# A fused Linformer-attention and MLP-mixer kernel: fixed program order with interleaved front steps, crossbar turns, and a down-projection from seven quadrant products

## The chip, the cores and the metric

One core of a Trainium2 chip runs the kernel. The metric is device time in microseconds (us) of one execution, as a median over runs. The profile is one execution, traced; its span (first to last instruction) is some 2 us shorter than the time of that execution. Engines: PE is TensorE, PEld its weight load, DVE VectorE, ACT ScalarE, POOL GpSimd, SP the queue of SyncE.

## The reference

Eight batches, each 1024 tokens x 512 channels (8 heads of 64). Attention first projects K and V along the sequence to 64 rows, so the scores of a head are 1024 x 64. The result goes through a token mixing (1024 to 256 to 1024, with a residual) and a channel MLP (512 to 1536 to 512, with a residual).

```python
k_proj = einsum('ks,bhsd->bhkd', E, k);  v_proj = einsum('ks,bhsd->bhkd', F, v)
attn   = softmax(q @ k_proj.T / 8)                  # max subtraction left out in both kernels
x      = (attn @ v_proj)  -> [B, S, H*D]
u      = x + (relu(x.T @ w_tok1) @ w_tok2).T        # token mixing
out    = u + relu(u @ w_ch1) @ w_ch2                # up- and down-projection
```

I call attention plus token mixing of a batch its *front*, and up- plus down-projection its *main* part.

## The kernel before

The body is written batch by batch; the framework's scheduler orders the instructions by priority and by what is ready. Operands are bf16, sums fp32 in PSUM.

```python
def attention(b):
    ...                                             # k, v, q loaded head by head, cast to bf16
    for hp in range(HP):                            # q: re-laid by a copy, turned on TensorE
        nc.any.tensor_copy(out=q2_sb[:, hp], in_=q_sb[...])
    for hp in range(HP):
        for sj in range(2):
            for ss in range(4):
                nc.tensor.transpose(qt_ps[:, ss * P : (ss + 1) * P], q2_sb[...], ident)
            nc.vector.tensor_copy(out=qT_sb[...], in_=qt_ps)
    for si in range(NSI):                           # V, then the same for K
        nc.tensor.matmul(vproj_ps, FT_sb[:, si, :], v_sb[:, :, si, :], ...)
    ...
            for ss in range(4):                     # denominators and outputs: 2 matmuls each
                nc.tensor.matmul(dn_ps[:, 2*ss : 2*ss+2], lhs, bd_ones, ...)
                nc.tensor.matmul(ou_ps[:, ss, :], lhs, vbd_sb[:, hp, :], ...)
    ...
def mixer(b, x_sb):
    ...                                             # token mixing: h_ps, u_ps, u_sb
                    nc.tensor.transpose(ut_ps[...], u_sb[:, sc, dc * P : (dc + 1) * P], ident)
                nc.vector.tensor_copy(out=uT_sb[...], in_=ut_ps)
    for sj in range(2):
        for cc in range(CC):                        # up: 96 matmuls of 512 columns a batch
            ...
            nc.any.tensor_relu(out=gT_sb[:, cc, s_lo : s_lo + S2], in_=gT_ps)
    for sc in range(SC):
        for cc in range(CC):                        # down: 96 matmuls of 512 columns a batch
            nc.tensor.matmul(g2_ps, gT_sb[:, cc, sc*P:(sc+1)*P], wc2_sb[:, cc, :], ...)
        nc.vector.tensor_add(out=o_sb, in0=g2_ps, in1=u_sb[:, sc, :])
        nc.sync.dma_start(out=..., in_=o_sb)
...
for b in range(B):
    if b + 1 < B: xs[b + 1] = attention(b + 1)
    mixer(b, xs[b])
```

Of the kernel before, what the change touches and what calls it, by code (L numbers as in the profile page):

```python
# [11 lines left out]
AX = mybir.AxisListType  # L12
ALU = mybir.AluOpType
ACT = mybir.ActivationFunctionType


@with_exitstack
def kernel(
# [14 lines left out]
    P = 128  # L33

# [5 lines left out]

    SC = S // P
    NSI = SC
    TC = DT // P
    DMC = DM // P
    CC = DC // P
    HP = H // 2
    scale = 1.0 / (D ** 0.5)
    S2 = S // 2

    const = ctx.enter_context(tc.tile_pool(name="const", bufs=1))  # L50
    wpool = ctx.enter_context(tc.tile_pool(name="weights", bufs=1))
    kv_pool = ctx.enter_context(tc.tile_pool(name="kv", bufs=2))
    attn_small = ctx.enter_context(tc.tile_pool(name="attn_small", bufs=4))
    attnT_pool = ctx.enter_context(tc.tile_pool(name="attnT", bufs=8))
    qT_pool = ctx.enter_context(tc.tile_pool(name="qT", bufs=2))
    mix_pool = ctx.enter_context(tc.tile_pool(name="mix", bufs=2))
    gT_pool = ctx.enter_context(tc.tile_pool(name="gT", bufs=1))
    out_pool = ctx.enter_context(tc.tile_pool(name="outp", bufs=4))
    psA = ctx.enter_context(tc.tile_pool(name="psA", bufs=8, space=bass.MemoryType.PSUM))
    dram_pool = ctx.enter_context(tc.tile_pool(name="dram", bufs=3, space=bass.MemoryType.DRAM))  # L60

    ident = const.tile([P, P], BF16)
    make_identity(nc, ident)
    bd_ones = const.tile([P, 2], BF16)
    nc.vector.memset(bd_ones, 0.0)
    nc.vector.memset(bd_ones[0:KP, 0:1], 1.0)
    nc.vector.memset(bd_ones[KP : 2 * KP, 1:2], 1.0)

    E_sb = const.tile([KP, S], BF16)
    nc.gpsimd.dma_start(out=E_sb, in_=E)  # L70
    F_sb = const.tile([KP, S], BF16)
    nc.gpsimd.dma_start(out=F_sb, in_=F)
    ET_sb = wpool.tile([P, SC, KP], BF16)
    FT_sb = wpool.tile([P, SC, KP], BF16)
    for si in range(NSI):
        ssl = slice(si, S, NSI)
        e_ps = psA.tile([P, KP], BF16, tag="ps", name="e_ps")
        nc.tensor.transpose(e_ps, E_sb[:, ssl], ident[:KP, :KP])
        nc.vector.tensor_copy(out=ET_sb[:, si, :], in_=e_ps)
        f_ps = psA.tile([P, KP], BF16, tag="ps", name="f_ps")  # L80
        nc.tensor.transpose(f_ps, F_sb[:, ssl], ident[:KP, :KP])
        nc.vector.tensor_copy(out=FT_sb[:, si, :], in_=f_ps)

    def attention(b):
        k_sb = kv_pool.tile([P, H, NSI, D], BF16, tag="k_sb", name="k_sb")
        v_sb = kv_pool.tile([P, H, NSI, D], BF16, tag="v_sb", name="v_sb")
        for h in range(H):
            rr = "(p si) d -> p si d"
            nc.gpsimd.dma_start(out=k_sb[:, h, :, :], in_=k[b, h].rearrange(rr, p=P))  # L89
            nc.gpsimd.dma_start(out=v_sb[:, h, :, :], in_=v[b, h].rearrange(rr, p=P))  # L90

        q_sb = kv_pool.tile([P, H, NSI, D], BF16, tag="q_sb", name="q_sb", bufs=1)
        for h in range(H):
            nc.gpsimd.dma_start(  # L94
                out=q_sb[:, h, :, :], in_=q[b, h].rearrange("(p si) d -> p si d", p=P)
            )
        q2_sb = kv_pool.tile([P, HP, NSI, 2, D], BF16, tag="q2_sb", name="q2_sb", bufs=1)
        for hp in range(HP):
            nc.any.tensor_copy(  # L99
                out=q2_sb[:, hp],  # L100
                in_=q_sb[:, 2 * hp : 2 * hp + 2].rearrange("p j si d -> p si j d"),
            )
        qT_sb = qT_pool.tile([P, HP, S], BF16, tag="qT_sb", name="qT_sb")
        for hp in range(HP):
            for sj in range(2):
                qt_ps = psA.tile([P, S2], BF16, tag="ps", name="qt_ps")
                for ss in range(4):
                    si = sj * 4 + ss
                    nc.tensor.transpose(  # L109
                        qt_ps[:, ss * P : (ss + 1) * P],  # L110
                        q2_sb[:, hp, si, :, :].rearrange("p j d -> p (j d)"),
                        ident,
                    )
                nc.vector.tensor_copy(  # L114
                    out=qT_sb[:, hp, sj * S2 : (sj + 1) * S2], in_=qt_ps
                )

        vproj_ps = psA.tile([KP, H, D], F32, tag="ps", name="vproj_ps")
        for si in range(NSI):
            nc.tensor.matmul(  # L120
                vproj_ps, FT_sb[:, si, :], v_sb[:, :, si, :],
                start=(si == 0), stop=(si == NSI - 1),
            )
        vbd_sb = attn_small.tile([P, HP, 2 * D], BF16, tag="vbd_sb", name="vbd_sb")
        nc.gpsimd.memset(vbd_sb, 0.0)
        for hp in range(HP):
            nc.vector.tensor_copy(out=vbd_sb[0:KP, hp, 0:D], in_=vproj_ps[:, 2 * hp, :])
            nc.vector.tensor_copy(  # L128
                out=vbd_sb[KP : 2 * KP, hp, D : 2 * D], in_=vproj_ps[:, 2 * hp + 1, :]
            )  # L130

        kproj_ps = psA.tile([KP, H, D], F32, tag="ps", name="kproj_ps")
        for si in range(NSI):
            nc.tensor.matmul(
                kproj_ps, ET_sb[:, si, :], k_sb[:, :, si, :],
                start=(si == 0), stop=(si == NSI - 1),
            )
        kproj_sb = attn_small.tile([KP, H, D], BF16, tag="kproj_sb", name="kproj_sb")
        nc.vector.tensor_copy(out=kproj_sb, in_=kproj_ps)
        kprojT_sb = attn_small.tile([P, HP, KP], BF16, tag="kprojT_sb", name="kprojT_sb")  # L140
        for hp in range(HP):
            tp_ps = psA.tile([P, KP], BF16, tag="ps", name="tp_ps")
            nc.tensor.transpose(
                tp_ps,
                kproj_sb[:, 2 * hp : 2 * hp + 2, :].rearrange("k j d -> k (j d)"),
                ident[:KP, :KP],
            )
            nc.vector.tensor_copy(out=kprojT_sb[:, hp, :], in_=tp_ps)

        x_sb = mix_pool.tile([P, SC, DM], BF16, tag="x_sb", name="x_sb")  # L150

        for sj in range(2):
            slo = sj * S2
            attns = []
            for hp in range(HP):
                sco_ps = psA.tile([P, S2], F32, tag="ps", name="sco_ps")
                nc.tensor.matmul(
                    sco_ps[0:KP, :], kprojT_sb[0:D, hp, :],
                    qT_sb[0:D, hp, slo : slo + S2], start=True, stop=True,
                )  # L160
                nc.tensor.matmul(  # L161
                    sco_ps[KP : 2 * KP, :], kprojT_sb[D : 2 * D, hp, :],
                    qT_sb[D : 2 * D, hp, slo : slo + S2], start=True, stop=True,
                )
                attnT_sb = attnT_pool.tile([P, S2], BF16, tag="attnT_sb", name="attnT_sb")
                nc.scalar.activation(out=attnT_sb, in_=sco_ps, func=ACT.Exp, scale=scale)  # L166
                attns.append(attnT_sb)
            for hp in range(HP):
                h0 = 2 * hp
                attnT_sb = attns[hp]  # L170
                dn_ps = psA.tile([P, 8], F32, tag="ps", name="dn_ps")
                ou_ps = psA.tile([P, 4, 2 * D], F32, tag="ps", name="ou_ps")
                for ss in range(4):
                    lhs = attnT_sb[:, ss * P : (ss + 1) * P]
                    nc.tensor.matmul(  # L175
                        dn_ps[:, 2 * ss : 2 * ss + 2], lhs, bd_ones, start=True, stop=True
                    )
                    nc.tensor.matmul(  # L178
                        ou_ps[:, ss, :], lhs, vbd_sb[:, hp, :], start=True, stop=True
                    )  # L180
                rdn = attn_small.tile([P, 8], F32, tag="rdn", name="rdn")
                nc.vector.reciprocal(out=rdn, in_=dn_ps)
                nc.vector.tensor_tensor(  # L183
                    out=x_sb[:, sj * 4 : sj * 4 + 4, h0 * D : (h0 + 2) * D]
                    .rearrange("p s (j d) -> p s j d", j=2),
                    in0=ou_ps.rearrange("p s (j d) -> p s j d", j=2),
                    in1=rdn.rearrange("p (s j) -> p s j", j=2)[:, :, :, None]
                    .to_broadcast([P, 4, 2, D]),
                    op=ALU.mult,
                )  # L190
        return x_sb
# [70 lines left out]
    for b in range(B):  # L262
        if b + 1 < B:
            xs[b + 1] = attention(b + 1)
# [32 lines left out]
```

## Time and profile before

| | before |
|---|---|
| time, median of 4 runs | 572.56 us (571.37 to 573.18) |
| span of the profile | 570.8 us |
| until the first up-projection | 85.2 us |
| one batch in the steady part | 64.7 us |
| busy share PE / DVE / ACT | 89% / 37% / 31% |

The page's table of 40 slices, before (each digit is a tenth; a slice is 14.3 us). PE is at 0.9 and more from the seventh slice on, at full clock; the six slices ahead of that are lower. The 9 at the head of the clock row says too much: the trace has no record of the clock before 24.5 us, and the table counts that time as full, but 128-column matmuls there start every 107 ns, as where the record says half clock, and not every 56 as later.

```profile
PE   1540889999999999998999999999999999999997
PEclk9975889999999999999999999999999999999999
```

The chain of waits, before (start, length, what). It returns to the same piece every 64.7 us. `gT_ps` is the up-, `g_ps` the down-projection.

```profile
85.20 20.96 PE gT_ps L233 x96
106.16 20.73 PE g_ps L242 x96
...
214.57 20.96 PE gT_ps L233 x96
235.53 20.73 PE g_ps L242 x96
...
269.40 3.45 PE h_ps L198 x16
...
279.47 20.96 PE gT_ps L233 x96
```

96 matmuls in 20.73 us and 16 in 3.45 us are 216 ns from one start to the next. I call this interval the *pitch*. It is the thing to add up for TensorE: the durations in the profile (379 ns for the same matmuls) overlap.

The timeline of TensorE, before (start, length, instruction, count). The 32 transposes take 1.95 us to the end of the last one (itself 0.22 us), so they start every 56 ns, each with a weight load of its own. The two score matmuls of a pair (L157, L161) use different quarters of the array and start within 10 ns of each other. From the last output matmul to the first score matmul it is 140 ns, where the starts ahead of it follow each other by 30 to 50.

```profile
256.09 1.95 PE L109 MATMUL qt_ps<-ident,q_sb 128*128 128x128 bf16 x32
...
266.14 0.22 PE L178 MATMUL ou_ps<-vbd_sb,attnT_sb 128*128 128x128 bf16 x1
266.28 0.40 PE L157 MATMUL sco_ps<-qT_sb,kprojT_sb 64*64 64x512 bf16 x1
266.29 0.40 PE L161 MATMUL sco_ps<-qT_sb,kprojT_sb 64*64 64x512 bf16 x1
```

### The profile page before, as it was taken

The page shows a single profiled execution, that of the slowest core. Times are in us where ns is not written, and L with a number is a line of the kernel's source. Part 1 is how long each engine was busy: PE and PEld are TensorE (multiplying, and loading weights), DVE is VectorE, ACT ScalarE, POOL GpSimd, SP SyncE. Part 2 cuts the span into 40 slices and gives each one's busy share as a digit, 9 for nine tenths or more (in the row PEclk, how much of TensorE's full clock was granted, in tenths as well). Part 3 has the DMA queues.
Part 4 walks back from the last instruction along what each step waited for, and adds up shares of the span by engine and source line. Part 5 has one row for each costly group of instructions (what it writes and reads, how often), then busy time and mean ns, then how long its engine had stood idle before and what let it go on. Part 6 is the DMA issues. An engine that isn't in the chain of part 4 may idle for free.

```text
span 570.8 us, 7698 instructions
## 1 busy us (share of the span) xinstructions
PE 509.8 (89%) x3120; PEld 259.4 (45%) x3120; DVE 210.4 (37%) x524; ACT 175.9 (31%) x288; POOL 110.9 (19%) x212
## 2 busy tenths in 40 slices
PE   1540889999999999998999999999999999999997
PEld 0330454454544454445544454445544454445443
DVE  1440571137502572028602563027601563025012
ACT  0221336305260235304260235404261034500720
POOL 8608871006200360006200260000000000000000
PEclk9975889999999999999999999999999999999999
DMA  9999992129502390028601391020001200020012
GB/s 135 208 208 202 201 201 44 38 92 151 91 0 79 102 186 4 27 103 134 109 1 73 94 185 19 20 102 28 1 1 69 80 2 0 18 94 38 1 55 92
DMA packets 39555, 46.90 MB, mean 82 GB/s; under 512 B 4192, under 2 KB 30304, under 8 KB 39520
## 3 DMA queue, kind: packets, MB, share of 16 engines
q0 software_dynamic: 30304, 29.63, 32.4%
q1 hardware_dynamic: 9216, 16.78, 7.5%
q8 instruction: 24, 0.39, 0.3%
q14 instruction: 11, 0.09, 0.1%
HBM read 59.24 MB, written 16.78 MB: 133 GB/s over the span
## 4 chain that ended last, share of the span: by engine, by line
PE 71%; DVE 14%; DMA 6%; POOL 5%; issue 2%; ACT 1%; DVEq 0%; ACTq 0%; POOLq 0%
PE gT_ps L233 29%; PE g_ps L242 29%; DVE u_sb L213 6%; PE h_ps L198 5%; DMA wc_sb<-in_moe_w_ch_dram 4%; DVE qT_sb L114 2%; PE ou_ps L178 2%; PE ut_ps L219 2%; POOL v_sb L90 2%; POOL q_sb L94 2%; PE u_ps L209 2%; POOL k_sb L89 1%; DVE x_sb L183 1%; PE dn_ps L175 1%; DVE vbd_sb L128 1%
## 5 line engine op out<-in xcount | busy, mean ns | idle before, releaser
L233 PE MATMUL gT_ps<-uT_sb,wc_sb 128*128 128x512 bf16 x768 | 169.0, 379 | 0.0
L242 PE MATMUL g_ps<-wc_sb,gT_sb 128*128 128x512 bf16 x768 | 167.1, 379 | 0.0
L238 ACT ACTIVATE gT_sb<-gT_ps 128x512 bf16<-128x512 f32 x184 | 109.0, 597 | 111.6 <-PE gT_ps L233 110.5
L247 DVE TENSOR_TENSOR o_sb<-g_ps,u_sb 128x512 f32<-128x512 f32 x64 | 44.3, 692 | 267.7 <-PE g_ps L242 267.7
L242 PEld LDWEIGHTS <-gT_sb 128*128 128x128 bf16 x768 | 75.1, 98 | 90.7
L233 PEld LDWEIGHTS <-wc_sb 128*128 128x128 bf16 x768 | 74.8, 98 | 90.7 <-issue 3.8
L90 POOL DMA_DIRECT2D v_sb<-in_v_dram x64 | 34.7, 545 | 203.2 <-PE vproj_ps L120 188.5
L99 ACT COPY q_sb<-q_sb 128x1024 bf16<-128x1024 bf16 x23 | 23.1, 1044 | 133.8 <-PE qt_ps L109 109.8
L166 ACT ACTIVATE attnT_sb<-sco_ps 128x512 bf16<-128x512 f32 x64 | 33.0, 602 | 61.2 <-PE sco_ps L161 61.2
L109 PE MATMUL qt_ps<-ident,q_sb 128*128 128x128 bf16 x256 | 19.5, 242 | 34.4 <-ACT q_sb L99 34.4
L213 DVE TENSOR_TENSOR u_sb<-u_ps,x_sb 128x512 bf16<-128x512 f32 x64 | 39.0, 683 | 21.2 <-PE u_ps L209 21.2
L183 DVE TENSOR_TENSOR x_sb<-ou_ps,rdn 128x512 bf16<-128x512 f32 x64 | 41.7, 681 | 1.7
L89 POOL DMA_DIRECT2D k_sb<-in_k_dram x64 | 34.6, 554 | 14.9 <-DMA wc_sb<-in_moe_w_ch_dram 6.8
L94 POOL DMA_DIRECT2D q_sb<-in_q_dram x64 | 34.0, 534 | 10.1 <-issue 5.3
L109 PEld LDWEIGHTS <-q_sb 128*128 128x128 bf16 x256 | 17.6, 109 | 37.1 <-ACT q_sb L99 35.5
L114 DVE COPY qT_sb<-qt_ps 128x512 bf16<-128x512 bf16 x64 | 23.0, 417 | 19.2 <-PE qt_ps L109 19.1
L175 PE MATMUL dn_ps<-bd_ones,attnT_sb 128*128 128x2 bf16 x256 | 27.4, 171 | 2.8 <-ACT attnT_sb L166 1.5
L178 PE MATMUL ou_ps<-vbd_sb,attnT_sb 128*128 128x128 bf16 x256 | 29.8, 221 | 0.0
L198 PE MATMUL h_ps<-x_sb,wt_sb 128*128 128x512 bf16 x128 | 29.7, 386 | 0.0
L209 PE MATMUL u_ps<-hT_sb,wt_sb 128*128 128x512 bf16 x128 | 28.9, 379 | 0.0
L175 PEld LDWEIGHTS <-attnT_sb 128*128 128x128 bf16 x256 | 20.0, 96 | 16.2 <-ACT attnT_sb L166 10.8
L219 PE MATMUL ut_ps<-ident,u_sb 128*128 128x128 bf16 x256 | 21.5, 221 | 5.1 <-DVE u_sb L213 4.6
(46 smaller groups left out, 260.0 us busy)
## 6 DMA issues: line engine op xcount, KB each, us to landing
out_dram<-o_sb SPq DMA_DIRECT2D x64, 256.0 KB, 2.0
k_sb<-in_k_dram POOLq DMA_DIRECT2D x64, 128.0 KB, 4.9
v_sb<-in_v_dram POOLq DMA_DIRECT2D x64, 128.0 KB, 4.9
q_sb<-in_q_dram POOLq DMA_DIRECT2D x64, 128.0 KB, 4.9
wc_sb<-in_moe_w_ch_dram POOLq DMA_DIRECT2D x2, 1536.0 KB, 18.8
wt_sb<-in_moe_w_tok_dram POOLq DMA_DIRECT2D x2, 512.0 KB, 7.4
E_sb<-in_E_dram POOLq DMA_DIRECT2D x1, 128.0 KB, 3.1
F_sb<-in_F_dram POOLq DMA_DIRECT2D x1, 128.0 KB, 3.4
```

Source lines behind the costliest of these rows:

```text
L90: nc.gpsimd.dma_start(out=v_sb[:, h, :, :], in_=v[b, h].rearrange(rr, p=P))
L94: nc.gpsimd.dma_start(out=q_sb[:, h, :, :], in_=q[b, h].rearrange("(p si) d -> p si d", p=P))
L175: nc.tensor.matmul(dn_ps[:, 2 * ss : 2 * ss + 2], lhs, bd_ones, start=True, stop=True)
L178: nc.tensor.matmul(ou_ps[:, ss, :], lhs, vbd_sb[:, hp, :], start=True, stop=True)
L183: nc.vector.tensor_tensor(out=x_sb[:, sj * 4 : sj * 4 + 4, h0 * D : (h0 + 2) * D] .rearrange("p s (j d) -> p s j d", j=2), in0=ou_ps.rearr ...
L198: nc.tensor.matmul(h_ps, wt1_sb[:, sc, tc_i * P : (tc_i + 1) * P], x_sb[:, sc, :], start=(sc == 0), stop=(sc == SC - 1),)
L209: nc.tensor.matmul(u_ps, wt2_sb[:, tc_i, sc::NSI], hT_sb[:, tc_i, :], start=(tc_i == 0), stop=(tc_i == TC - 1),)
L213: nc.vector.tensor_add(out=u_sb[:, sc, :], in0=u_ps, in1=x_sb[:, sc, :])
L233: nc.tensor.matmul(gT_ps, wc1_sb[:, dc, cc * P : (cc + 1) * P], uT_sb[:, dc, s_lo : s_lo + S2], start=(dc == 0), stop=(dc == DMC - 1),)
L238: nc.any.tensor_relu(out=gT_sb[:, cc, s_lo : s_lo + S2], in_=gT_ps)
L242: nc.tensor.matmul(g2_ps, gT_sb[:, cc, sc * P : (sc + 1) * P], wc2_sb[:, cc, :], start=(cc == 0), stop=(cc == CC - 1),)
L247: nc.vector.tensor_add(out=o_sb, in0=g2_ps, in1=u_sb[:, sc, :])
```

## The change

The intent: keep TensorE fed by a program order written by hand, and give it less to do.

1. **Fixed order.** The scheduler is switched off. The front of batch b+1 is a generator of 31 steps (the loop shares out 33); the main loop of batch b takes one step after about every 1.3 of its own, beside batch 0, where it starts later, after every one.
2. **Crossbar turns.** q and u of batches 1 to 7 are transposed by DMA, on SP's queue, not by TensorE.
3. **Seven products.** The down-projection is split in 2 x 2 quadrants and made from seven products (Winograd's form of Strassen's scheme). 24 sums of activations a batch come on, and sums of the PSUM results; the sums of weights are made once.
4. **Smaller things.** K and V project into different column halves of the array. A column of ones beside V gives the denominators. K, V, q are loaded in large DMAs. The first batch's front goes by head pairs, as its loads land.

```diff
+    ctx.enter_context(tc.manual_schedule())
...
+    def turn_q(b):
+            nc.sync.dma_start_transpose(out=st["qT", b][:, hs]..., in_=st["q", b][:, hs]...)
...
+            nc.tensor.matmul(kv_ps[0:KP, 0:n], EFT[:, si, 0:KP], st["k", b][:, hs, ds], **f)
+            nc.tensor.matmul(kv_ps[KP:P, 0:n], EFT[:, si, KP:P], st["v", b][:, hs, ds], **f)
...
+    def front(b):
+        turn_q(b)
+        yield
+        for j in range(4):
+            kv_mm(b, kv_ps, slice(0, H), range(2 * j, 2 * j + 2))
+            if j < 3:
+                yield
+        kv_vec(b, kv_ps, kprojs, slice(0, H))
+        ...
+        yield
+        kt_step(b, kprojs, kT, slice(0, H), front_ps)
+        yield
+        ats = {0: score_step(b, 0, kT, front_ps)}
+        yield
+        for h in range(H):
+            if h + 1 < H:
+                ats[h + 1] = score_step(b, h + 1, kT, front_ps)
+            ou_step(b, h, ats.pop(h))
+            yield
+        ...                                   # token mixing in steps; u turned by the crossbar
+    def front_first():                        # batch 0, by head pairs
+        attn(0)
+        for hp in range(1, HP):
+            attn(hp)
+            mix(hp - 1)
...
+        def sums(i):                          # after every fourth up-projection group
+            nc.vector.tensor_add(out=s1, in0=a21, in1=a22)
+            nc.vector.tensor_sub(out=s2, in0=s1, in1=a11)
+            nc.vector.tensor_sub(out=s3, in0=a11, in1=a21)
+            nc.vector.tensor_sub(out=s4, in0=a12, in1=s2)
...
+                    if n % 8 in (1, 4, 6):
+                        nc.vector.tensor_relu(out=o, in_=g_ps)
+                    else:
+                        nc.scalar.activation(out=o, in_=g_ps, func=ACT.Relu)
...
+    def down_wino(b):                         # P1..P7: 6 matmuls of 256 columns each, 4 row blocks
...
+            if b == 0 and WINO_DOWN:
+                down_weights()                # four sums of weights, on VectorE
```

## The prediction

> **What bounds it now.** TensorE, and before it a cold start. The 40-slice table shows PE 0.9 to 1.0 busy from slice 7 on, at full clock. The chain of waits repeats every 64.7 us per batch (192.2, 257.0, 321.9). In one period 96 up-projection matmuls take 20.96 us and 96 down-projection ones 20.73 (216 ns from start to start at 512 columns); the other 23 us are attention and token mixing with short waits. 85.2 us pass until the first up-projection; the last batch has no front beside it (51.8 us); the end costs 3.6.
>
> **What changes, per batch (pitches read in the timeline).**
> - Down: 96 matmuls of 512 columns become 4 x 7 x 6 = 168 of 256. 128-column transposes, each with its own weight load, start every 54 ns, so weight loading should not limit: 108 ns each, 18.2 us. Gain 2.5 us.
> - 64 TensorE transposes (3.4 us, plus waits) go to the DMA crossbar.
> - K and V projections use different column halves: if they overlap as the two score matmuls already do (8 ns apart), 3.5 us become 1.8.
> - The 32 denominator matmuls vanish (0.8 us).
> - Waits between stages (some 10 us: 64.7 less 54 of matmul pitches) should be filled, as front steps are spread between main steps.
> TensorE per batch: up 20.8, down 18.2, token mixing 6.9, K/V 1.8, scores 1.7, outputs 1.8, kT 0.4 = 51.6 us; the last batch 39.
> - Added: DVE gets 24 sums of 128x512 bf16 and 24 PSUM adds of 256 columns. The Trainium skill, "VectorE: DVE Perf Modes" (perf-mode tier table), gives such a tensor_tensor 2x; none is in this trace (its PSUM adds take 0.68 us at 512). Estimate from that page: (256+151)/0.96 = 0.42 us, so 10 + 10 us; with the rest about 41 us of DVE in 52, nearer 95% in the up half.
> - Small tile modes (scores, K/V, kT) now sit between full-size matmuls, some 30 switches a batch. The skill, "TensorEngine Tiling (Array Packing)" (Key Properties), says a mode change drains TensorE; here outputs to scores costs some 0.1 us over the usual pitch. Estimate 1 to 2 us a batch.
>
> **Start.** The queue moves 205 GB/s. Batch 0's q, k, v and the token weights (4.2 MB) land near 23 us; the front now runs by head pairs in short, partly cold pieces: first up-projection near 45 us instead of 85. Up weights land in time (30 us), batch 1's K/V near 48, before their step.
>
> **Sum.** 45 + 7 x 51.6 + 39 = 445; mode switches 10; waits for DVE, PSUM buffers, sums at the up/down edge and crossbar turns 1.5 us a batch = 12; difference weights 2; end 3.5. Prediction **472 us**, 450 to 505. Faster by over 2%: 0.95; within 2%: 0.03; slower: 0.02. About 40 us come from the start, 60 from the steady batches; the seven products alone are some 20.
>
> **Right or wrong shows in:** start of the first up matmul (45); the chain's period per batch (53 to 55); start-to-start of 256-column matmuls (108 ns; wrong if weight loads set 120+); mean of the sums (0.42 against 0.69 us); DVE's share (about 75%); PE waits released by DVE, or by the crossbar DMA.
>
> **What would make it wrong.** Sums at 1x: DVE becomes the limit, +5 us a batch. Crossbar turns slow, or stuck behind outputs on SP's queue: PE waits for uT at each batch's start. A fixed order stalls all of TensorE when one front step is late. K/V not overlapping adds 12 us.

## The result, and the profile after

The changed kernel takes **507.94 us** (507.00 to 508.68, 4 runs), against 572.56 us: ratio 0.8877, 95% interval 0.8860 to 0.8893. Ratios here are from fast runs alone, so not quite the ratio of the quoted medians. The direction and the forecast of TensorE's own work were right; the time lies above the top of the predicted range (505 us).

The table of 40 slices, after (a slice is now 12.6 us):

```profile
PE   2667997899989999999989999999989999999996
PEclk9996999899999999999999999999999999999999
```

The chain of waits, after. `g_ps` is now the up-projection, `al`, `be` and `ga` are products of the down-projection. The first up-projection starts at 53.6 us. Batch 1's starts at 117.8, batch 2's at 175.0, batch 3's at 232.3: 64.2 us for batch 0, then 57.24 us each. The fixed order breaks the up-projection into groups of 4 and 8.

```profile
53.63 12.98 PE g_ps L368 x60
...
85.46 0.88 DVE dT L466
...
117.79 5.18 PE g_ps L368 x24
...
175.03 5.18 PE g_ps L368 x24
...
232.27 5.18 PE g_ps L368 x24
...
460.86 19.87 PE g_ps L368 x92
```

The prediction can be laid beside this part by part (spans; its 10 us for switches spread over seven batches, its 12 us for waits over eight, its 2 us for weights put on batch 0):

| part | before | predicted | after |
|---|---|---|---|
| until the first up-projection | 85.2 | 45 | 53.6 |
| batch 0, main part with front 1 | 64.6 | 56.5 | 64.2 |
| next six batches | 375.6 | 327 | 343.1 |
| last main part and end | 45.4 | 44 | 44.3 |
| sum | 570.8 | 472.5 | 505.2 |

So 31.6 us came from the start and 33 us from the batches. (The six batches gain 32.5 us, not six times the 7.5 us of a steady period: before, the last of the six takes only 51.8 us, as no attention is left to do beside it.) The missing 32.7 us are 8.6 at the start, 7.7 in batch 0 and 16.1 in the six batches after it.

What TensorE does in one batch of the steady part, as count x measured pitch (216 ns at 512 columns, 109 at 256, 56 at 128 or 130):

| us per batch | before | after |
|---|---|---|
| up 96 x 512 | 20.7 | 20.7 |
| down | 20.7 | 18.3 |
| token mixing 32 x 512 | 6.9 | 6.9 |
| K and V projection | 3.5 | 1.7 |
| scores | 1.7 | 1.7 |
| outputs and denominators | 2.6 | 1.8 |
| turns of q and u | 3.6 | 0 |
| kT | 0.1 | 0.2 |
| sum of pitches | 59.9 | 51.4 |
| period | 64.7 | 57.2 |
| rest: all that is not matmul pitch | 4.8 | 5.8 |

The matmul side came out as predicted to 0.2 us. The rest did not: it was to shrink and it grew. The timeline of TensorE, after, shows what it consists of. In brackets stands the idle time before a piece and what ended it.

```profile
243.05 0.38 PE L159 MATMUL kv_ps<-k_sb,EFT 128*64 128x512 bf16 x1
243.05 0.38 PE L160 MATMUL kv_ps<-v_sb,EFT 128*64 128x512 bf16 x1
243.37 1.04 PE L368 MATMUL g_ps<-uT,wc 128*128 128x512 bf16 x4
244.79 0.40 PE L165 MATMUL kt_ps<-ident,kprojs 64*128 64x64 bf16 x8 [0.39 <-DVE kprojs L150]
245.13 1.04 PE L368 MATMUL g_ps<-uT,wc 128*128 128x512 bf16 x4
246.68 0.40 PE L179 MATMUL sco<-qT,kT 64*64 64x512 bf16 x2 [0.51 <-DVE kT L170]
247.01 1.90 PE L368 MATMUL g_ps<-uT,wc 128*128 128x512 bf16 x8
248.84 0.40 PE L179 MATMUL sco<-qT,kT 64*64 64x512 bf16 x2
249.18 0.40 PE L192 MATMUL ou_ps<-vbd,attnT 128*128 128x130 bf16 x4
```

Two things are in it. First, open waits: kT transposes and scores come one group of four matmuls after what they depend on, and that is too soon. Second, a surcharge at each change of the tile shape even where nothing waits: from the last score pair of 248.84 to the outputs at 249.18 it is 0.34 us, while a pair's pitch is 0.216. The Trainium skill, "TensorEngine Tiling (Array Packing)" (Key Properties), says that changing the tiling mode drains TensorE. Measured here: 0.09 to 0.12 us each, 26 a batch in the changed kernel, 2.8 us by the gaps in the trace. Before, the same count gives 6 changes, some 0.8 us of the 4.8. So the interleaving did fill about 1 us of waits, from 4.0 to 3.0, but it added 2 us of changes of shape. Of the 3.0 us that are left for waits, the waits view of the period from 232.27 to 289.5 names 2.3 (who waits <- for whom: us in total, times, longest):

```profile
PE ou_ps L192 <- DVE x_sb L199: 0.8, 1, 0.8
PE sco L179 <- DVE kT L170: 0.5, 1, 0.5
PE ou_ps L192 <- ACT g L377: 0.4, 1, 0.4
PE kt_ps L165 <- DVE kprojs L150: 0.4, 1, 0.4
PE h_ps L243 <- DVE x_sb L199: 0.2, 1, 0.2
```

VectorE is not the limit by throughput. The busy times of stretches, after, for the up half and the down half of that batch (length; then PE, PEld, DVE, ACT, POOL, each with its instruction count; granted clock; share and GB/s of DMA), put it at 20.48 of 30.73 us (67%), not at the predicted "nearer 95%":

```profile
232.27:263.00 30.73, 28.64 (x166) 11.40 (x164) 20.48 (x44) 13.29 (x23) 2.67 (x3) 1.00 0.92 154
263.00:289.50 26.50, 26.18 (x202) 20.39 (x204) 18.47 (x42) 3.33 (x7) 7.79 (x12) 1.00 0.41 101
```

The feared 1x rate of the sums did not occur either. In the groups of instructions, after (count | us busy, mean ns of one | idle before), they take 0.415 to 0.425 us at 512 elements, as the Trainium skill's "VectorE: DVE Perf Modes" (perf-mode tier table) led to expect:

```profile
L346 DVE TENSOR_TENSOR S<-g 128x512 bf16<-128x512 bf16 x48 | 19.9, 415 | 0.0
```

In batch 0 the waits view (53.6 to 117.8) has one large entry more, the sums of weights:

```profile
PE ga L419 <- DVE dT L466: 3.3, 1, 3.3
PE ou_ps L192 <- DVE x_sb L199: 2.1, 2, 1.7
...
```

### The profile page after: what moved, and what is told of

It reads as the page before. It is cut to its first block, busy times and chain, and to the rows that moved or that the text cites. A ratio compares the mean times of both kernels' runs of the same rounds, so it can differ in the third digit from the quotient of the medians.

```text
span 505.2 us, 8059 instructions
## 1 busy us (share of the span) xinstructions
PE 458.3 (91%) x3139; PEld 273.2 (54%) x3160; DVE 321.3 (64%) x708; ACT 142.4 (28%) x259; POOL 96.2 (19%) x143
## 4 chain that ended last, share of the span: by engine, by line
PE 80%; DVE 12%; ACT 3%; DMA 2%; issue 1%; POOL 1%; POOLq 0%; ACTq 0%; DVEq 0%
PE g_ps L368 28%; PE be L419 13%; PE al L419 8%; PE ga L419 8%; PE h_ps L243 5%; PE u_ps L255 4%; PE ou_ps L192 4%; DVE x_sb L199 3%; PE sco L179 3%; PE kv_ps L159 3%; DMA q_sb<-in_q_dram 2%; DVE g L375 2%; PE h_ps L300 1%; PE u_ps L309 1%; DVE rdn L198 1%
## 5 line engine op out<-in xcount | busy, mean ns | idle before, releaser
L368 PE MATMUL g_ps<-uT,wc 128*128 128x512 bf16 x768 | 182.7, 380 | 0.0
L368 PEld LDWEIGHTS <-wc 128*128 128x128 bf16 x768 | 69.5, 98 | 80.5 <-issue 13.1
L377 ACT ACTIVATE g<-g_ps 128x512 bf16<-128x512 f32 x120 | 71.6, 597 | 137.7 <-PE g_ps L368 137.7
L419 PEld LDWEIGHTS <-S 128*128 128x128 bf16 x768 | 75.4, 98 | 25.1 <-issue 3.8
L375 DVE TENSOR_SCALAR g<-g_ps 128x512 bf16<-128x512 f32 x72 | 49.6, 689 | 56.1 <-PE g_ps L368 56.1
L419 PEld LDWEIGHTS <-g 128*128 128x128 bf16 x576 | 56.3, 98 | 17.8
L419 PE MATMUL be<-dT,S 128*128 128x256 bf16 x384 | 53.0, 275 | 0.2 <-DVE V L442 0.2
L419 PE MATMUL al<-wc,g 128*128 128x256 bf16 x384 | 52.4, 273 | 0.6
L184 ACT ACTIVATE attnT<-sco 128x512 bf16<-128x512 f32 x64 | 37.6, 595 | 29.5 <-PE sco L179 29.5
L255 PE MATMUL u_ps<-R_sb,wt 128*128 128x512 bf16 x105 | 31.8, 379 | 0.0
## 6 DMA issues: line engine op xcount, KB each, us to landing
wc<-in_moe_w_ch_dram POOLq DMA_DIRECT2D x4, 384.0 KB, 12.6
v_sb<-in_v_dram POOLq DMA_DIRECT2D x4, 256.0 KB, 10.4
```

What stands on the lines that cost most here:

```text
L184: nc.scalar.activation(out=at, in_=sco, func=ACT.Exp, scale=scale)
L255: nc.tensor.matmul(u_ps, wt2[:, t, s::SC], st["R", b][:, t, :], start=(t == 0), stop=(t == TC - 1),)
L368: nc.tensor.matmul(g_ps, wc1[:, dc, cc * P : (cc + 1) * P], uT[:, 4 * sh : 4 * sh + 4, dc, :], start=(dc == 0), stop=(dc == DMC - 1),)
L375: nc.vector.tensor_relu(out=o, in_=g_ps)
L377: nc.scalar.activation(out=o, in_=g_ps, func=ACT.Relu)
L419: nc.tensor.matmul(acc[:, 0:HF], l, r, start=start and c == 0, stop=c == CH - 1, skip_group_check=True,)
```

## The experiments

Theory A: the rest of 5.8 us a batch is about half changes of tile shape and half waits for single results of VectorE and ScalarE that the fixed order asks for too early. Its rivals: the whole rest is VectorE's queue (B), or VectorE has nothing to do with it (C). Theory S for the start: a chain of latencies in a fixed order; rival L: loads or the slow clock. All kernels are edits of the changed kernel. "Period" is the distance between the first up-projection matmuls of two successive batches in the steady part of the trace; the first up-projection is taken here from its first matmul, which is 53.5 us in the trace of the changed kernel (the chain above has 53.6). Differences of runs from different calls are taken from the ratios, times 571.7 us.

### Control

> Control: the changed kernel unaltered, on the chip of the runs beside it. Both theories: 505 to 511 us, first up-projection near 53.6 us, period 57.2 us per batch.

508.15 us, ratio 0.8887; first up-projection at 54.8 us, batch 0 takes 64.4 us, period 57.25 us. The period differs by 0.01 us between the two traces of this kernel. The start varies more: in the nine traces with the first front unchanged, the first up-projection starts between 53.5 and 56.0 us (median 54.8). The trace of the result is the earliest of them, so the 8.6 us missing at the start are the least that any of them shows.

### K and V projection in one step

```diff
-            kv_mm(b, kv_ps, slice(0, H), range(2 * j, 2 * j + 2))
+            kv_mm(b, kv_ps, slice(0, H), range(SC) if j == 3 else ())
```

> The K/V projection of a batch in one front step, not four: 6 fewer changes of the TensorE tile shape per batch, same work. Theory A (each change of tile shape costs TensorE some 0.1 us, 26 to 28 of them a batch): the period falls by about 0.6 us, the time by about 4 us (503 to 505). Rival B (the long pitches at these places are waits for VectorE's queue, changes of shape are free): no change within 1 us.

503.86 us, ratio 0.8809; period 56.57 us. The three other steps stay, empty. Six changes of shape fewer save 0.68 us a batch: 0.113 us each. The waits stayed the same. Theory A holds here, B doesn't.

### Scores of two heads in one step

```diff
-        ats = {0: score_step(b, 0, kT, front_ps)}
+        ats = {h: score_step(b, h, kT, front_ps) for h in (0, 1)}
         yield
         for h in range(H):
-            if h + 1 < H:
-                ats[h + 1] = score_step(b, h + 1, kT, front_ps)
             ou_step(b, h, ats.pop(h))
+            if h % 2 == 1 and h + 1 < H:
+                for k2 in (h + 1, h + 2):
+                    ats[k2] = score_step(b, k2, kT, front_ps)
             yield
```

> Scores of two heads in one front step: 8 fewer changes of tile shape per batch. Theory A: period down by some 0.9 us, time down by 6 to 7 us, to about 501. Rival B: no change, or a little slower, since two scores follow each other and the second exponential comes later.

509.97 us, ratio 0.8919; period 57.19 us. Theory A's 0.9 us did not show; the time is what rival B named. But by the gaps in the trace the changes of shape around the scores did cost less, from 1.8 to 0.8 us a batch, and the outputs, no longer preceded by a score pair, now wait more for the single output buffer that VectorE empties. The waits view of one period (292.17 to 349.35): 1.6 us, 0.8 before.

```profile
PE ou_ps L192 <- DVE x_sb L199: 1.6, 4, 0.5
...
```

### All relus on ScalarE

```diff
-                    if n % 8 in (1, 4, 6):
+                    if False:
```

> All 24 relu evictions a batch on ScalarE, none on VectorE (9 x 0.69 us less on VectorE per batch). Theory A (of 5.7 us excess a batch some 2.4 us are waits for VectorE): period down by 1 to 2 us, time down by 7 to 14 us. Rival B (all 5.7 us are VectorE's queue): period down by 4 us or more, time down by 25 us or more. Rival C (VectorE has nothing to do with it): unchanged, or slower where exponentials now queue behind relus on ScalarE.

502.88 us, ratio 0.8793; period 56.17 us. 1.08 us a batch: the waits for the output buffer and for ScalarE's relu go (0.8 and 0.4 before, 0.2 and none now), those for kprojs and kT stay (waits view from 287.59 to 343.75). Rivals B and C fall. Theory A's time is missed too: 5.4 us by the ratios, not 7 to 14, as the period only reaches the lower edge of its range and batch 0 gains nothing (64.4 us).

```profile
PE sco L179 <- DVE kT L170: 0.5, 1, 0.5
PE kt_ps L165 <- DVE kprojs L150: 0.4, 1, 0.4
PE ou_ps L192 <- DVE x_sb L199: 0.2, 1, 0.2
...
```

### The sums of activations in batch 0 only

The result is wrong (relative error 0.64).

```diff
-            st["S", b] = [
+            st["S", b] = st["S", 0] if b else [
...
-            sums = up_sums(b)
+            sums = up_sums(b) if b == 0 else None
```

> Wrong result on purpose from batch 1 on: the 24 sums are made for batch 0 only and used by all, so the seven products' matmuls stay and 10 us of VectorE a batch go. Theory A (waits for VectorE are about 2.4 us of the 5.7 us excess): period down by 1.5 to 2.5 us, time down by 10 to 16 us. Rival B (the whole excess is VectorE's queue): down by 30 us or more.

502.3 us, ratio 0.8775; period 56.21 us. Taking 10 us of VectorE away saves 1.04 us a batch, no more than taking 6.2 us of relus away. It is less than Theory A expected, in the time too (6.4 us by the ratios, not 10 to 16): what VectorE's load costs ends near 1 us, and the waits for kT and kprojs (0.5 and 0.4 us) are as long as before.

### Sums of weights spread over the first up-projection

```diff
+        dw = down_weights() if b == 0 and WINO_DOWN else iter(())    # now a generator, one sum each
         for i in range(CH):
+            next(dw, None)
...
-            if b == 0 and WINO_DOWN:
-                down_weights()
```

> The four difference weights (3.7 us of VectorE) are made one by one during the up-projection of batch 0, not in one block before its down-projection. If the 3.5 us wait of TensorE at that place is all they cost: time down by 3 to 4 us. If batch 0's extra 7 us are a VectorE backlog that the block only shares in: down by 1 us or less, or by 5 or more.

504.29 us, ratio 0.8821, 3.8 us less than the control by the ratios, as the first outcome has it. Batch 0 takes 59.5 us instead of 64.4 (traces), so most of its surplus came with this one block of four instructions. The 4.9 us are more than the wait of 3.3 us. In the trace of the changed kernel the clock is at half from 86.1 to 92.9 us, right after that wait; 256-column matmuls start every 213 ns there instead of 109, which adds some 1.7 us by the gaps. In the trace with the weights spread, the clock stays full. (That the wait makes the clock fall is not shown: in the trace of the four edits below, which spread the weights too, it still falls in batch 0, for 3.4 us.) Of the 2.2 us that batch 0 still takes over a period, some 1.7 are longer waits: 4.0 us in the waits view, 1.9 of them for the output buffer, against 2.3 in a steady period. Beside batch 0 the front's steps follow each other more closely; whether that makes the waits longer was not tried.

### The first front, pipelined

The same instructions; between the stages of one head pair stand stages of its neighbours.

```diff
-        attn(0)
-        for hp in range(1, HP):
-            attn(hp)
-            mix(hp - 1)
...
+        A(0); K(0); S_(0); O(0); O(1); A(1)    # A: K/V projection, turn q; K: kT; S_: scores; O: output
+        for hp in range(1, HP):
+            K(hp)
+            A(hp + 1)                          # at the last one: the loads of batch 1
+            S_(hp); Hm(hp - 1, 0); O(2 * hp); Hm(hp - 1, 1)
+            if hp > 1: T(hp - 2)
+            O(2 * hp + 1); U(hp - 1)           # Hm, U: token mixing; T: turn u
+        Hm(HP - 1, 0); Hm(HP - 1, 1); T(HP - 2); U(HP - 1); T(HP - 1)
```

> The first batch's front with the same instructions, but the stages of one head pair put between those of the next. Theory S (from 18 us on the start is a chain of latencies in a fixed order, loads are there): first up-projection at 42 to 47 us instead of 53.6, time down by 7 to 11 us. Rival L (loads or the slow clock bound it): first up-projection within 2 us of 53.6.

496.82 us, ratio 0.8688, 11.4 us less than the control by the ratios; first up-projection at 43.1 us; period unchanged (57.25). Theory S holds, with an addition. The stretches of the start, first the changed kernel, then this one (columns as above; the number after POOL is the granted clock):

```profile
9.00:53.60 44.60, 31.23 (x313) 23.46 (x314) 18.53 (x44) 13.01 (x27) 10.10 (x13) 0.89 1.22 199
```

```profile
9.00:43.00 34.00, 25.35 (x310) 18.95 (x311) 17.31 (x44) 12.99 (x27) 10.81 (x14) 1.00 1.23 205
```

The same matmuls were 31.2 us busy in the one and 25.4 us in the other. So of 10.6 us, some 6 are TensorE's busy time, and the rest is less idling. The clock column (0.89 and 1.00) needs care: it counts the time before the first record of the clock, at 28.1 and 25.1 us, as full, though 128-column matmuls start every 107 ns there and every 56 ns after it. Counted as half clock, it makes 38.3 us at half clock before the first up-projection in the changed kernel and 25.1 us here. What that is worth can be estimated from the other traces. In the nine with the first front unchanged the time at half clock goes from 37.1 to 47.2 us, and the first up-projection comes some 0.22 us later for each us of it (a straight line through the nine; 0.21 through the five traces with this front, from 24.1 to 27.2 us). By this estimate the clock accounts for about 3 of the 10.4 us between the two first up-projections, and the order for the rest; a run that changes one without the other was not made.

The loads moved at the same rate in both (199 and 205 GB/s) and were not the limit in the changed kernel, where the last piece of batch 0 landed at 25.5 us and TensorE waited 0.2 us for loads. With the front pipelined it waits 2.9 us for them.

### The plain down-projection

```diff
-WINO_DOWN = True
+WINO_DOWN = False
```

> The down-projection back to eight quadrant products (96 matmuls of 512 columns a batch), all else as changed. If the products are worth their matmul time, as predicted (2.5 us a batch, some 20 in all): 528 us. Theory A (the sums' waits, the difference weights and the wait at the up/down edge give much of it back): 507 to 518 us, with a period of 57 to 58.5 us.

512.17 us, ratio 0.8954; period 58.23 us, batch 0 60.0 us. The seven products are worth 3.8 us by the ratios, not the predicted 20. They take 2.4 us of pitch a batch off TensorE, and 1.0 us of it stays: with the plain form the rest is 4.4 us, with seven products 5.8. And batch 0 gives 4.4 us back for the weights. Against the run that spreads the weights, the plain form is 7.6 us slower by the ratios: so much are the products worth once their weights are out of the way. One period of the plain kernel in the waits view (289.97 to 348.2) has 1.0 us instead of 2.3:

```profile
PE kt_ps L165 <- DVE kprojs L150: 0.3, 1, 0.3
PE ou_ps L192 <- DVE x_sb L199: 0.3, 1, 0.3
PE sco L179 <- DVE kT L170: 0.2, 1, 0.2
PE h_ps L243 <- DVE x_sb L199: 0.2, 1, 0.2
```

### The scheduler's order

```diff
-    ctx.enter_context(tc.manual_schedule())
```

> The changed kernel without its fixed program order: the framework's scheduler orders the same instructions by its own priorities. If the order is what the gain rests on: over 530 us. If the order is worth little (the gain is matmul time taken away): within 10 us of 508.

492.04 us, ratio 0.8605: 16.1 us *faster* than with the fixed order, by the ratios. That is neither of the two outcomes that I had named. Instruction counts of TensorE and its weight loads, VectorE and ScalarE in the page are near equal or equal (708 on VectorE and 259 on ScalarE in both). Batch 0 takes 56.7 us (64.4 in the control), the next two periods 56.9, the later ones 54.7 to 55.4. In the period from 281.44 to 336.37 the waits view of TensorE is empty; of the 3.5 us of rest 2.7 are changes of shape by the gaps, of which there are 26 as in the fixed order, and the others gaps too small for that view. The timeline of TensorE shows what the scheduler did: five up-projection matmuls before kT, six before the first scores, where the fixed order has four.

```profile
292.69 1.25 PE L367 MATMUL g_ps<-uT,wc 128*128 128x512 bf16 x5
293.88 0.40 PE L164 MATMUL kt_ps<-ident,kprojs 64*128 64x64 bf16 x8
294.21 1.47 PE L367 MATMUL g_ps<-uT,wc 128*128 128x512 bf16 x6
295.68 0.40 PE L178 MATMUL sco<-qT,kT 64*64 64x512 bf16 x2
```

So the fixed order by itself costs time in this kernel, while its interleaved text, handed to the scheduler, serves well as a priority. The two periods of 56.9 us each have one wait of 1.7 us, of a down-projection product (`be`) for VectorE (o_sb, in the waits view from 112.18 to 226.01); the next period has 0.2 us of it, the later ones none. Why it is there was not followed.

### The turns back on TensorE

```diff
-        turn_q(b)
-        yield
+        for hp in range(HP):                  # 8 transposes, eviction by ScalarE
+            ...
+            yield
...
-                nc.sync.dma_start_transpose(out=st["uT", b]..., in_=st["u", b]...)
+                if s > 1:
+                    turn_u(b, s - 2)          # 8 transposes, eviction by ScalarE
...
-        n_front = 33
+        n_front = 37
```

> The turns of q and u of batches 1 to 7 back on TensorE (64 transposes a batch and their evictions on ScalarE), all else as changed, in the fixed order. Their pitch is 56 ns: 3.6 us a batch, 25 us over seven. If turns cost only that: 533 us, period 60.8 us. If evictions and waits come on top: 540 us or more. If they fill TensorE's waits: under 525 us.

550.63 us, ratio 0.9634, as the second outcome has it; period 62.97 us, batch 0 72.7 us. The crossbar is worth 42.7 us in this order, by far the largest single part: 3.6 us of pitch a batch and 2.1 us of further waits, 5.7 together, and 8 us in batch 0. In batch 0 one wait of 6.7 us (94.84 us in the timeline) is for an output buffer that VectorE empties only after eight sums and the block of weights, so not all of the 42.7 us is the turns' own; their pitch is 25 us of it. With the scheduler's order the turns on TensorE were not tried. The waits view of one period (315.78 to 378.75) names some of the further waits:

```profile
PE ou_ps L192 <- DVE x_sb L199: 1.5, 2, 1.3
PE ou_ps L192 <- ACT attnT L184: 0.7, 1, 0.7
PE ga L442 <- DVE S L369: 0.7, 1, 0.7
...
```

### Four edits together, in both orders

Pipelined start, K/V in one step, weights early, relus on ScalarE.

> Fixed order, with four of the edits that helped one by one: pipelined start (11.3 us), K/V in one step (4.3), weights early (3.9), relus on ScalarE (5.3), each the difference of its median to the control. If they address separate waits, they add up: 483 us, first up-projection at 42 to 44 us, period 55.5. If they share the same waits: 487 to 492.

481.04 us, ratio 0.8413 (0.8399 to 0.8428); first up-projection at 42.6 us, batch 0 60.3, period 55.48. The savings add up. It beats both kernels.

The same without the line that fixes the order:

> The same four edits, with the scheduler's order in place of the fixed one. The scheduled kernel has no wait of TensorE over 0.2 us in most of its periods, so only the start and the changes of tile shape are left to gain: first up-projection at 42 to 46 us, period 54 to 55, 475 to 482 us. If the scheduler undoes the written interleaving of the start: near 490.

481.73 us, ratio 0.8425: no better. The periods are 53.9 to 56.2 us and batch 0 takes 54.6, but the first up-projection starts at 52.6 us: the scheduler did not keep the written interleaving of the start. As far as these two runs show, a fixed order pays at the start and a scheduled one later; a kernel with both was not made.

### Empty steps, and pairs once more

An empty step before and one after the kT transposes (`yield` twice, `n_front = 35`) on top of the four edits:

> best_fixed with one empty front step before the kT transposes and one after, so that a group of up-projection matmuls stands between each and what it waits for. If the waits at kprojs (0.4 us) and kT (0.5 us) are a matter of place alone: period 54.6 (55.5 before), about 475 us. If the front, now squeezed into smaller intervals, waits elsewhere instead: period unchanged.

486.46 us, ratio 0.8513, slower; period 56.32, which neither outcome had named. The two waits did vanish: the entries for kprojs and kT are gone from the waits view of 274 to 329 us. But later steps, pressed together, wait for more, and the down-projection now waits for a sum:

```profile
PE ou_ps L192 <- DVE x_sb L199: 0.9, 2, 0.7
PE ga L454 <- DVE S L379: 0.7, 1, 0.7
PE h_ps L245 <- DVE x_sb L199: 0.4, 1, 0.4
...
```

The profiled run also had a single wait of 9.3 us for the turned q in batch 0: that turn landed 18.5 us after its issue (median 4.6), with 2 MB of K and V for batch 2 loading at the same time. This is the slow crossbar turn that the prediction named as a risk. The run is the slowest of its six (492.94 us) and not the one to compare.

Scores by pair on top of the four edits:

> best_fixed with scores by pair: 8 fewer changes of tile shape. If scores_by_pair brought nothing because its saving (0.9 us a batch by Theory A) came back as waits for the single output buffer behind a busy VectorE, then here, with the relus off VectorE, some of it stays: period 54.6 to 55.2, 475 to 479 us. If changes of tile shape at the scores cost nothing: period unchanged at 55.5.

481.35 us, ratio 0.8414, equal to the four edits; period 55.31 instead of 55.48, between the two outcomes named. Only a fifth of the 0.9 us stays even with the relus off VectorE, so the load of VectorE is not all of what took it back: by the gaps in the trace, the eight groups of outputs, which now follow up-projection matmuls directly, still start 1.1 us a batch late.

Both:

> Both edits. If they are separate: period 53.8 to 54.2, 469 to 473 us.

485.03 us, ratio 0.8483; period 56.17, far from the forecast. The two do not add to a gain; the empty steps cost what they cost before.

## Why the prediction was right or wrong

- **The bound and the direction: right.** TensorE sets the period before and after, and the change is faster by 11%.
- **TensorE's own work: right.** Predicted 51.6 us a batch, and 51.4 by counts and pitches. 256-column matmuls start every 109 ns (108 predicted), so weight loads don't limit here. K and V do overlap. Sums take 0.42 us.
- **"Waits between stages (some 10 us ...) should be filled": wrong, the step that failed in the batches.** The size was a mis-sum: the pitches before add up to 59.9 us, not 54, so there were only 4.8 us to fill. (54 is about what is left without the turns, the denominators and half of K and V, 53.8: perhaps these were counted twice, but the record does not show how the 54 was made.) And on the whole they were not filled: 4.8 became 5.8, as about 1 us of waits went and 2 us of changes of shape came. In the sum of the prediction all this stands as 2.9 us a batch (10 us over seven batches, and 1.5). What a steady batch gained is matmul time taken away (8.5 us), less 1.0 given back.
- **"mode switches 10": mis-sized.** Right in kind, 2.8 us a batch by the gaps, some 20 us over seven batches; taking six away saved 0.113 us each.
- **"waits ... 1.5 us a batch": mis-sized.** 3.0 us measured. Not because VectorE is full (67% in the up half), but because the fixed order stands on single results: the relus or sums ahead of x_sb cost 1.05 us (taken away in two experiments), and the waits view has 0.9 us for the places of kT and kprojs (other places removed these waits, but others came for them). The other 1 us was not assigned. The scheduler's order, with the same work, has at most 0.2 us for kprojs and none of the others in any period.
- **"First up-projection near 45 us": wrong by 8.6.** The loads were there, as predicted (the last piece of batch 0 at 25.5 us; near 23 predicted). The short pieces were taken for a small matter; in fixed order they were a chain of latencies, with TensorE at half clock for more of the time. Put between each other, the same instructions reach the first up-projection at 43.1 us.
- **"difference weights 2": mis-sized.** Moving them saved 4.9 us of batch 0: a wait of 3.3 us and a fall of the clock after it.
- **"the seven products alone are some 20": wrong.** 3.8 us: the term was the pitch saved (2.4 us a batch), without what the added sums cost in waits (some 1.4 us a batch) and in batch 0.
- **Crossbar turns "3.4 us, plus waits": right in kind.** 5.7 us a batch, and 42.7 us in all, of which 8 us fall in batch 0, where the block of weights has a share in the wait.

Not settled: why the waits of batch 0 are longer, why the scheduler's order waits for VectorE in its early periods, and, but for the estimate above, the share of the clock in the start.

## What to carry to other kernels

Add up matmul starts, not busy times, before calling the remainder "waits to be filled"; and count what the interleaving itself adds, here 0.11 us for each change of tile shape and a stall of all of TensorE for each step placed one group too early. Before you fix an order by hand, run the same text with the scheduler on: it is a one-line experiment, and here it was 16 us faster (after the four edits the two orders tied). Fewer multiplications are worth only what is left after their additions have found a place: 3.8 us of a hoped-for 20 here, 7.6 with the weights spread, while moving transposes off TensorE brought 43 in this order.

## What the Trainium skill lacked or had wrong

- "TensorEngine Tiling (Array Packing)", Key Properties, says that a change of tiling mode drains TensorE but gives no time. Here it is 0.09 to 0.12 us each by the gaps, and 0.113 us by taking six a batch away (57.25 to 56.57 us).
- "TensorE: Matmul & The Clock Gate", Back-to-back issue gap, gives some 81 ns per matmul at 128 columns and 131 ns at 512 as the sustained rate with weight loads. Here each matmul has its own weight load and they start every 56 ns at 128 columns, 109 at 256 and 216 at 512. The page's isolated figures (about 56 and 216) fit; its "sustained" ones do not.
- "DMA: Bandwidth & Descriptors", DMA Transpose (X-bar), has no time from issue to landing for a turn of this size within SBUF (bandwidths stand elsewhere on the page, and a time for a single 128x128 block on the page "VectorE: DVE Perf Modes"). Here a turn of u (256 KB) lands 3.1 us after its issue and one of q (512 KB) after 4.7 us (medians), with up to 6.2 us for q in the trace of the changed kernel and 18.5 us once beside other loads.
- "VectorE: DVE Perf Modes", perf-mode tier table: its 2x for bf16 sums held (0.42 us for 512 elements, 0.95 us for 1536).
